# Weight conversion during the attention: intermediate words in a PSUM bank, high halves on GpSimd

## The chip, the cores and the metric

The kernel runs on one core of a Trainium2 chip. The metric is the device time of one execution in microseconds (us); lower is better. The kernel before takes 1587.08 us, the median of 3 runs (1586.88 to 1588.7).

## The reference

Three stages follow each other: an attention with hashed buckets, a feed-forward layer with a rational activation, and eight experts weighted by a normalised gate. The weights w_in and w_out of the second stage arrive as 64-bit floats, because a 32-bit array is multiplied by a 64-bit scalar when they are set up.

```python
def _attn_ref(q, k, v, proj):
    mask = q_bucket[:, :, :, None] == k_bucket[:, :, None, :]
    scores = np.where(mask, scale * np.matmul(q, k.transpose(0, 1, 3, 2)), -1e9)
    attn = np.exp(scores - np.max(scores, axis=-1, keepdims=True))
    attn = attn / (np.sum(attn, axis=-1, keepdims=True) + 1e-09)
    return np.matmul(attn, v).astype(np.float32)
...
def _moe_ref(x, w_in, w_out, a, b):
    h = x @ w_in
    P = a[0] + a[1] * h + a[2] * h * h + a[3] * h * h * h
    Q = 1.0 + np.abs(b[0]) * np.abs(h) + np.abs(b[1]) * h * h
    return ((P / (Q + 1e-06)) @ w_out).astype(np.float32)
```

## The kernel before

Every fp32 operand is split into a high half (fp32r) and a low half (the rest), and a product is three matmuls: high by high, high by low, low by high.

**The attention** (L683 to L762) runs 48 iterations: 16 heads, each with 3 groups of 256 query rows. An iteration issues two `scores` (TensorE into the two-bank tiles of `ps_s`, then VectorE L285 takes the row minimum out of PSUM and ScalarE L286 the exponential), three `trans` (four TensorE transposes L308 into a one-bank tile `pt`, a ScalarE copy of the high half into `pth` by L106, a VectorE subtraction into `ptl` by L109), one `values` (twelve matmuls L323 into a one-bank tile `av`, ScalarE L106 and VectorE L334 take it out), and `norm` (VectorE L291 and L292, GpSimd L294). Once per head `prep_head_a` fills four one-bank tiles `tp` (taken out by ScalarE L246) and `prep_head_b` two one-bank tiles `hp` (taken out by VectorE L260, which writes the mask bits). All of `tp`, `hp`, `pt` and `av` come from the same four PSUM banks: `bank(name)` at L89 has one tag with `bufs=4`, and per head they are 18 tiles.

**The weight conversion** of a 64-bit weight tile of 128x512 numbers (`prep_weights` L188, path `one`) has these steps: ScalarE takes the absolute value of the upper words into `c` (L169), GpSimd clips it (L170), VectorE builds two 32-bit floats out of the raw words in four steps (`narrow_b`, L180 to L183), GpSimd adds them into `c` (L186), ScalarE copies the high half of `c` into the weight slot (L208, by the helper `act_copy` at L106), and GpSimd writes the low half (L210, by `pool_lo` at L103). The tile `c` has two buffers (`conv`, L87), so the L169 of one conversion waits until the last step (L103) of the conversion two before has read `c`.

Thirty-two tiles are converted: eight during the attention (the dictionary `wprep` at L718 places them at iterations 35, 38, 41 and 44, one of w_in and one of w_out each), the other 24 during the second stage. The flag `bits_in_psum` tells the two apart: it is False for the eight (L719) and True for the 24 (L784). During the second stage the intermediate words `pc` lie in the PSUM bank `sum_bank(3, "bits")`; during the attention `pc` is `c` itself.

**What orders the work.** During the attention a planner orders each engine's instructions: an instruction's rank is its place in the program, and one that is ready when its engine would otherwise idle, by the planner's own estimate of times, is taken ahead of its place if its tile can be had. So the eight conversions are spread over the first 215 us although the program places them at iterations 35 to 44. From L806 on (`manual_schedule`) the order is the one that is written. Each engine executes its queue in order. The second stage starts with `gemm1` (L354) on the first four pairs of converted weights.

Of the kernel before, what the change touches and what calls it, by code (L numbers as in the profile page):

```python
# [35 lines left out]
def kernel(  # L36
# [52 lines left out]
    def bank(name):  # L89
        return ps.tile([P, 512], F32, tag="b", bufs=4, name=name)  # L90
# [4 lines left out]
    def split(eng_hi, eng_lo, hi, lo, src):  # L95
        eng_hi(hi, src)
        eng_lo(lo, src, hi)
# [4 lines left out]
    def pool_lo(lo, src, hi):  # L102
        pool.tensor_tensor(lo, src, hi.bitcast(F32), ALU.subtract)  # L103

    def act_copy(o, src):
        act.activation(o, src, AF.Copy)  # L106
# [38 lines left out]
    def load_weights(m, c):  # L145

        if c >= (NA_W if wide else NA_W // 2) + E * EF // 2:
            return
        if c < NA_W and wide:
            src, f, nf = (moe_w_in, moe_w_out)[m].bitcast(I32), c, 1  # L150
        elif c < NA_W // 2 and not wide:
            src, f, nf = (moe_w_in, moe_w_out)[m], 2 * c, 2
        else:
            e, f = divmod(2 * (c - (NA_W if wide else NA_W // 2)), EF)
            src, nf = (w1, w2)[m][e], 2
        w = 2 // nf if src.dtype == I32 else 1
        if m == 0:
            r = raw.tile([P, KC, 2 * P], src.dtype, tag="ra", name="ra")
            sp.dma_start(r, src[:, f * P * w:(f + nf) * P * w].rearrange("(c p) f -> p c f", p=P))
        else:  # L160
            r = raw.tile([P, nf, 2 * DM // nf], src.dtype, tag="rb", name="rb")
            sp.dma_start(r, src[f * P:(f + nf) * P, :].rearrange("(f p) d -> p f d", p=P))
        raws[m, c] = r

    def narrow_a(bits):


        c = conv.tile([P, bits.shape[1]], F32, tag="c", name="c")
        act.activation(c, bits[:, :, 1].bitcast(F32), AF.Abs)  # L169
        pool.tensor_scalar(c, c, F64_HIGH, F64_LOW, ALU.min, ALU.max)  # L170
        return c

    def narrow_b(bits, c):


        ci = c.bitcast(I32)
        pc = sum_bank(3, "bits") if bits_in_psum else c
        pi = pc.bitcast(I32)
        low, high = bits[:, :, 0], bits[:, :, 1]
        dve.tensor_scalar(pi, ci, 5, 2, ALU.logical_shift_left, ALU.logical_shift_right)  # L180
        dve.scalar_tensor_tensor(high, high, -0x40000000, pi, ALU.bitwise_and, ALU.bitwise_or)
        dve.tensor_scalar(pi, high, -0x800000, None, ALU.bitwise_and)
        dve.scalar_tensor_tensor(low.bitcast(F32), low.bitcast(U32), 2.0 ** -52, pc, ALU.mult, ALU.mult)  # L183

    def narrow_c(bits, c):
        pool.tensor_tensor(c, bits[:, :, 0].bitcast(F32), bits[:, :, 1].bitcast(F32), ALU.add)  # L186

    def prep_weights(m, i):  # L188

        if i >= NW:  # L190
            return
        one = wide and i < NA_W
        c, j = (i, 0) if one else divmod(i - NA_W, 2) if wide else divmod(i, 2)
        if wide and not one:
            c += NA_W
        r = raws[m, c]
        t = wslots[(i % NSLOT) // 4].tile([P, 2, 512], F32R, tag=f"w{'ab'[m]}{i % NSLOT}", name="w" + "ab"[m])
        slots[m, i] = tuple(t[:, k].rearrange("p (c f) -> p c f", c=KC) if m == 0 else t[:, k] for k in range(2))
        if one:
            bits = (r.rearrange("p c f -> p (c f)") if m == 0 else r[:, 0]).rearrange("p (n t) -> p n t", t=2)  # L200
            n = narrow_a(bits)
            yield
            narrow_b(bits, n)
            yield
            narrow_c(bits, n)
            load_weights(m, c + 2)
            yield
            act_copy(t[:, 0], n)  # L208
            yield
            pool_lo(t[:, 1], n, t[:, 0])  # L210
            return
        if m == 0:
            split(pool_hi, pool_lo, t[:, 0].rearrange("p (c f) -> p c f", c=KC),
                  t[:, 1].rearrange("p (c f) -> p c f", c=KC), r[:, :, j * P:(j + 1) * P])
        else:
            split(pool_hi, pool_lo, t[:, 0], t[:, 1], r[:, j])
        if j == 1:
            load_weights(m, c + 2)
# [500 lines left out]
    bits_in_psum = False  # L719
    for it in range(NG + VLAG):  # L720
# [39 lines left out]
        if it in wprep:  # L760
            for m in range(2):
                list(prep_weights(m, wprep[it]))  # L762
# [11 lines left out]
    def sum_bank(j, name):  # L774

        return ps_f.tile([P, 512], F32, tag="f" if j < 3 else "c", bufs=3 if j < 3 else 1, name=name)
# [7 lines left out]
    bits_in_psum = True  # L784
# [21 lines left out]
    with tc.manual_schedule(engines={mybir.EngineType.PE, mybir.EngineType.Activation, mybir.EngineType.DVE,  # L806
# [3 lines left out]
        for s in range(NS + QF):  # L810
            n = s - NS
# [19 lines left out]
            if n < 0:  # L831
                go(new)
            narrowing = [prep_weights(m, i) for m, i in preps.get(s, ())]
            narrowing = [w for w in narrowing if go(w)]
            for w in old_w:
# [116 lines left out]
```

## Time and profile before

| | |
|---|---|
| median of 3 runs | 1587.08 us |
| the profiled execution | 1589.4 us, of which the span is 1587.6 us |
| TensorE busy | 1536.8 us (97%) |
| VectorE busy | 1199.3 us (76%) |
| ScalarE busy | 622.1 us (39%) |
| GpSimd busy | 938.9 us (59%) |
| mean granted TensorE clock | 0.994 |

The attention takes the first 290 us of the span, the second stage goes on to about 575 us, the experts take the rest. The busy shares are averages over these stages: VectorE is nearly full in the first and the second and is idle for about a third of the last. What the change is worth must therefore be read from the first 290 us alone: from the timeline of each engine, from the windows, and from the distance between the same step of successive heads.

### The profile page before, as it was taken

Reading aid. Unit: us, or ns where it says so; the run is one execution under the profiler, and the core shown is the slowest. Engines: PE = TensorE matmul, PEld = TensorE weight load, DVE = VectorE, ACT = ScalarE, POOL = GpSimd, SP = SyncE. Lnnn points to the kernel's source line nnn. Section 1 sums busy time; section 2 is a strip of 40 time slices with the busy share of each in tenths; the row PEclk is TensorE's granted clock in tenths of the full one; section 3 lists DMA queues with packets and bytes.
Section 4 is the critical chain, followed back from the end, with each engine's and each line's share of the span. In section 5 each row is a group of like instructions: output and inputs, shape, how many; then the busy total and the mean of one; then the engine's idle time right before and its main releaser. Section 6 shows DMA issues by size and latency. Waiting matters only on the chain.

```text
span 1587.6 us, 22241 instructions
## 1 busy us (share of the span) xinstructions
PE 1536.8 (97%) x8071; PEld 1355.8 (85%) x8071; DVE 1199.3 (76%) x2116; ACT 622.1 (39%) x1167; POOL 938.9 (59%) x1165
## 2 busy tenths in 40 slices
PE   5989999899999999999999999999999999999999
PEld 4888889687777877889899999989899998989898
DVE  7989999799999984886666766676666666666665
ACT  4878888788777842111111111111111111111111
POOL 6777875577777976456644653564465356436530
PEclk8999999999999999999999999999999999999999
DMA  5322221021212000101010110101011001101002
GB/s 170 86 83 79 81 70 25 14 67 54 66 53 67 14 27 27 41 27 40 27 41 27 41 40 27 36 32 40 27 40 41 27 28 40 40 27 40 14 1 80
DMA packets 49406, 71.85 MB, mean 45 GB/s; under 512 B 4368, under 2 KB 35088, under 8 KB 49296
## 3 DMA queue, kind: packets, MB, share of 16 engines
q1 hardware_dynamic: 48432, 68.85, 14.1%
q8 instruction: 64, 1.05, 0.3%
q10 hardware_dynamic: 864, 1.57, 0.3%
q14 instruction: 46, 0.38, 0.1%
HBM read 59.79 MB, written 3.15 MB: 40 GB/s over the span
## 4 chain that ended last, share of the span: by engine, by line
PE 65%; DVE 2%; ACT 0%; issue 0%; DVEq 0%; ACTq 0%
PE accb L599 33%; PE prod L534 29%; PE acca L405 2%; PE h L354 1%; PE lp L635 0%; DVE t L470 0%; DVE t L473 0%; DVE c L559 0%; DVE part L417 0%; DVE gl L555 0%; ACT xb L106 0%; DVE t L480 0%; ACT gh L554 0%; DVE t L484 0%; DVE csum L676 0%
## 5 line engine op out<-in xcount | busy, mean ns | idle before, releaser
L534 PE MATMUL prod<-xb,ww 128*128 128x384 f32 x2688 | 481.7, 336 | 1.8 <-ACT m L106 1.3
L599 PE MATMUL accb<-wb,gh 128*128 128x512 f32 x1536 | 475.7, 391 | 2.9 <-ACT osum L106 2.5
L534 PEld LDWEIGHTS prod<-xb,ww 128*128 128x128 f32 x2688 | 469.8, 188 | 8.0 <-ACT m L106 1.6
L610 DVE SCALAR_TENSOR_TENSOR osum<-accb,gp,osum 128x512 f32<-128x512 f32 x336 | 251.7, 749 | 127.7 <-PE accb L599 126.0
L599 PEld LDWEIGHTS accb<-wb,gh 128*128 128x128 f32 x1536 | 287.0, 188 | 60.9 <-ACT osum L106 2.9
L599 PE MATMUL accb<-wb,gl 128*128 128x512 f32 x768 | 300.9, 392 | 0.4 <-DVE gl L555 0.4
L100 POOL TENSOR_SCALAR wb<-rb 128x512 fp32r<-128x512 f32 x64 | 40.2, 627 | 405.8 <-PE accb L599 405.8
L554 ACT ACTIVATE gh<-c 128x384 fp32r<-128x384 f32 x256 | 134.3, 526 | 352.5 <-DVE c L559 352.1
L106 ACT ACTIVATE m<-prod 128x384 f32<-128x384 f32 x64 | 31.5, 492 | 457.9 <-PE prod L534 457.9
L599 PEld LDWEIGHTS accb<-wb,gl 128*128 128x128 f32 x768 | 144.2, 188 | 32.0 <-DVE gl L555 1.7
L555 DVE SCALAR_TENSOR_TENSOR gl<-c,gh 128x384 fp32r<-128x384 f32 x256 | 165.2, 645 | 1.3 <-ACT gh L554 0.9
L559 DVE TENSOR_TENSOR c<-prod,u 128x384 f32<-128x384 f32 x192 | 106.6, 558 | 61.7 <-PE prod L534 54.1
L354 PE MATMUL h<-xh,wa 128*128 128x512 f32 x384 | 126.7, 392 | 3.4 <-DVE tu L377 3.4
L405 PE MATMUL acca<-gh,wb 128*128 128x512 f32 x384 | 126.4, 391 | 2.8 <-DVE part L417 1.7
L109 DVE TENSOR_TENSOR ptl<-pt,pth 128x512 fp32r<-128x512 f32 x144 | 94.5, 682 | 19.1 <-ACT pth L106 18.3
L559 DVE TENSOR_TENSOR c<-prod,m 128x384 f32<-128x384 f32 x64 | 35.7, 558 | 92.4 <-PE prod L534 92.4
L103 POOL TENSOR_TENSOR ww<-ra,ww 128x256 fp32r<-128x256 f32 x128 | 95.4, 746 | 10.7
L294 POOL TENSOR_SCALAR e<-e,rs 128x768 f32<-128x768 f32 x96 | 88.8, 937 | 20.8 <-DVE rs L292 11.3
L308 PE MATMUL pt<-idr,e 128*128 128x128 f32 x576 | 83.0, 279 | 11.1 <-DVE ptl L109 4.9
L285 DVE TENSOR_SCALAR_CACHE_REDUCE e<-s 128x768 f32<-128x768 f32 x96 | 90.9, 949 | 2.1 <-PE s L278 1.7
L286 ACT ACTIVATE e<-e,nm 128x768 f32<-128x768 f32 x96 | 89.9, 936 | 3.8 <-DVE e L285 3.1
L354 PEld LDWEIGHTS h<-xh,wa 128*128 128x128 f32 x384 | 72.1, 188 | 22.4 <-DVE tu L377 5.9
(168 smaller groups left out, 2546.3 us busy)
## 6 DMA issues: line engine op xcount, KB each, us to landing
ra<-in_moe_w_dram SPq DMA_DIRECT2D x32, 512.0 KB
rb<-in_moe_w_dram SPq DMA_DIRECT2D x32, 512.0 KB
ra<-in_moe_w_in_dram SPq DMA_DIRECT2D x16, 512.0 KB
rb<-in_moe_w_out_dram SPq DMA_DIRECT2D x16, 512.0 KB
qkv<-in_q_dram SPq DMA_DIRECT2D x16, 192.0 KB
qkv<-in_k_dram SPq DMA_DIRECT2D x16, 192.0 KB
qkv<-in_v_dram SPq DMA_DIRECT2D x16, 192.0 KB
a<-a SPq DMA_DIRECT2D x16, 192.0 KB
```

Source lines behind the costliest of these rows:

```text
L103: pool.tensor_tensor(lo, src, hi.bitcast(F32), ALU.subtract)
L109: dve.tensor_tensor(lo, src, hi.bitcast(F32), ALU.subtract)
L285: dve.tensor_scalar(e[j], s[:, 0:S], BIG, None, ALU.min, ALU.min, accum_out=nm)
L286: act.activation(e[j], e[j], AF.Exp, bias=nm, scale=-1.0, accum_out=rs[:, j, 0:1])
L354: pe.matmul(hps, lhsT=a[:, c], rhs=x[:, c], start=m == 0, stop=m == 3 * KC - 1)
L405: pe.matmul(o, lhsT=l[:, js], rhs=r, start=f == 0 and m == 0, stop=f == QF - 1 and m == 2)
L534: pe.matmul(o, lhsT=w[:, i, c], rhs=x[:, j, c], start=n == 0, stop=n == 5)
L554: act.activation(gh, c, AF.Relu)
L555: low.append(lambda: dve.scalar_tensor_tensor(gl, c, 0.0, gh.bitcast(F32), ALU.max, ALU.subtract))
L559: dve.tensor_tensor(c, o, x, ALU.add)
L599: pe.matmul(o, lhsT=l[:, ts], rhs=r, start=n == 0 and m == 0, stop=n == 1 and m == 2)
L610: dve.scalar_tensor_tensor(d, o, gate["p"][:, n, e:e + 1], d, ALU.mult, ALU.add)
```

## The change

Two expressions change, and both act only while `bits_in_psum` is False, that is for the eight conversions during the attention. The intermediate words `pc` of `narrow_b`, which L180 writes, L181 reads, L182 writes again and L183 reads, lie in a tile of `bank("bits")`, one of the four banks that `tp`, `hp`, `pt` and `av` share, and no longer in `c`. And the high half of the converted tile is written by `pool_hi` (L100, GpSimd) where it was written by `act_copy` (L106, ScalarE).

```diff
         ci = c.bitcast(I32)
-        pc = sum_bank(3, "bits") if bits_in_psum else c
+        pc = sum_bank(3, "bits") if bits_in_psum else bank("bits")
         pi = pc.bitcast(I32)
...
-            act_copy(t[:, 0], n)
+            (act_copy if bits_in_psum else pool_hi)(t[:, 0], n)
             yield
             pool_lo(t[:, 1], n, t[:, 0])
```

## Rows read from the trace of the kernel before

**Rows 1.** Windows: stretch; busy us (count) per engine; granted clock, DMA share, GB/s.
```profile
240.00:260.00 20.00, 20.00 (x150) 18.09 (x149) 17.47 (x41) 17.77 (x38) 12.51 (x16) 1.00 0.19 45
...
285.00:300.00 15.00, 14.98 (x80) 12.63 (x81) 7.74 (x13) 8.37 (x15) 6.79 (x9) 1.00 0.00 1
```

**Rows 2.** Timeline (start us, us, instruction), VectorE: first mask-bit step of ten heads.
```profile
92.93 1.29 DVE L260 TENSOR_SCALAR bits<-hp,thr 44x512 fp32r<-44x512 f32 x2
...
110.95 1.29 DVE L260 TENSOR_SCALAR bits<-hp,thr 44x512 fp32r<-44x512 f32 x2
...
130.63 1.29 DVE L260 TENSOR_SCALAR bits<-hp,thr 44x512 fp32r<-44x512 f32 x2
...
146.75 1.29 DVE L260 TENSOR_SCALAR bits<-hp,thr 44x512 fp32r<-44x512 f32 x2
...
164.68 1.29 DVE L260 TENSOR_SCALAR bits<-hp,thr 44x512 fp32r<-44x512 f32 x2
...
180.79 1.29 DVE L260 TENSOR_SCALAR bits<-hp,thr 44x512 fp32r<-44x512 f32 x2
...
197.60 1.29 DVE L260 TENSOR_SCALAR bits<-hp,thr 44x512 fp32r<-44x512 f32 x2
...
212.81 0.82 DVE L260 TENSOR_SCALAR bits<-hp,thr 44x512 fp32r<-44x512 f32 x1
...
229.83 1.29 DVE L260 TENSOR_SCALAR bits<-hp,thr 44x512 fp32r<-44x512 f32 x2
...
260.51 1.29 DVE L260 TENSOR_SCALAR bits<-hp,thr 44x512 fp32r<-44x512 f32 x2
```

**Rows 3.** Timeline, four engines, one conversion's end; the last line another's.
```profile
111.41 0.63 ACT L106 ACTIVATE wa<-c 128x512 fp32r<-128x512 f32 x1 [2.50 <-POOL c L186]
...
112.11 1.29 POOL L103 TENSOR_TENSOR wa<-c,wa 128x512 fp32r<-128x512 f32 x1 [0.74 <-ACT wa L106]
...
113.44 0.69 ACT L169 ACTIVATE c<-ra 128x512 f32<-128x512 f32 x1 [0.48 <-POOL wa L103]
...
114.63 0.69 DVE L109 TENSOR_TENSOR ptl<-pt,pth 128x512 fp32r<-128x512 f32 x1 [2.40 <-ACT pth L106]
...
115.47 0.63 PE L308 MATMUL pt<-idr,e 128*128 128x128 f32 x4 [1.45 <-DVE ptl L109]
...
213.98 0.63 ACT L106 ACTIVATE wb<-c 128x512 fp32r<-128x512 f32 x1 [2.29 <-POOL c L186]
```

**Rows 4.** Windows, as rows 1: one microsecond after that end.
```profile
118.00:119.00 1.00, 1.00 (x5) 0.90 (x5) 1.00 (x4) 0.00 (x0) 0.00 (x0) 0.50 0.00 0
```

**Rows 5.** Windows, only instructions on tile c, then (300:520) on bits.
```profile
13.00:26.00 13.00, 8.19 (x8) 1.40 (x3) 5.25 (x5) 0.84 0.57 146
...
30.00:300.00 270.00, 22.17 (x24) 7.84 (x12) 17.61 (x18) 0.98 0.24 67
...
300.00:520.00 220.00, 66.28 (x96) 1.00 0.18 58
```

**Rows 6.** Line view: count, ns min/median/max, first and last start, form.
```profile
L180 DVE TENSOR_SCALAR c<-c x8: 405/893/1220, 13.6 to 177.7; 128x512 int32<-128x512 int32 x8
...
L100 POOL TENSOR_SCALAR wb<-rb x64: 617/619/922, 550.8 to 1523.9; 128x512 fp32r<-128x512 f32 x64
```

**Rows 7.** Timeline, TensorE: a wait at the start of the attention.
```profile
25.22 0.79 PE L277 MATMUL s<-b,a 128*128 128x512 f32 x1 [3.51 <-DVE e L285]
```

**Rows 8.** Timeline, TensorE and VectorE: banks' first writers, last readers; one conversion's span.
```profile
88.35 1.03 PE L308 MATMUL pt<-idr,e 128*128 128x128 f32 x8
...
90.85 0.39 PE L259 MATMUL hp<-a,pjr 128*108 128x256 f32 x2
...
91.55 1.28 DVE L109 TENSOR_TENSOR ptl<-pt,pth 128x512 fp32r<-128x512 f32 x2
...
107.81 0.89 DVE L180 TENSOR_SCALAR c<-c 128x512 int32<-128x512 int32 x1
...
141.34 1.42 DVE L183 SCALAR_TENSOR_TENSOR rb<-rb,c 128x512 f32<-128x512 uint32 x1
```

## The prediction

> **What bounds the kernel now.** The change touches only the eight conversions of the attention, so I read that stage and the way its end reaches the total. First the windows view: where the attention runs without conversions (240 to 260 us) TensorE is busy for all of the 20 us, VectorE for 17.47 and GpSimd for 12.51 [rows 1]; TensorE sets the pace there, with VectorE close behind. At the hand-over to the second stage (285 to 300 us) TensorE is busy for 14.98 of 15 us [rows 1]: the second stage's matmuls follow the attention's without a gap, and all they need of this stage is the attention's result and weights that are ready long before. So a microsecond won or lost in the attention reaches the end one for one.
>
> Second, the pace. The first mask-bit step of each head (L260) is a mark that comes once a head [rows 2]. From 229.83 to 260.51, with no conversion at work, two heads take 30.68 us, 15.34 each. With conversions the heads fall in two kinds. Five take 18.02, 19.68, 17.93, 16.81 and 17.02 us, 89.46 together, 17.89 each. Three others take 16.12, 16.11 and 15.21, 15.81 each [rows 2]. So a conversion costs about 0.5 us in a head of the second kind and 2.1 us more in one of the first.
>
> Third, the timeline of the engines shows what the first kind has. ScalarE comes to the copy of the high half (L106, wa<-c) and waits 2.50 us for GpSimd's sum (L186); the exponentials and pth copies stand behind it in its queue. Then VectorE waits 2.40 us for pth, and TensorE waits 1.45 us for VectorE to give back a bank [rows 3]. There are five such waits between 91 and 214 us, the last of 2.29 us [rows 3], one in each of the five slow heads. Behind the one shown TensorE's granted clock falls to 0.50, that is 1.2 of its 2.4 GHz [rows 4], after TensorE had been idle; that is in the head of 19.68 us.
>
> **The change, part by part.**
>
> *The copy leaves ScalarE.* Eight copies of 0.63 us [rows 3] and their waits for L186 go; the step follows L186 on the same engine. In the heads of 16.81 and 17.02 us nothing else of a conversion stands on ScalarE. They should fall to the pace of the second kind: 33.83 - 2 x 15.81 = 2.2 us won. In the other three, L169 of a later conversion stands soon behind the copy and waits for GpSimd's last step L103 on the same buffer of c (0.48 us in the row [rows 3]). ScalarE now comes to that L169 up to 2.5 us earlier, while L103 ends about as late as before, so a part of the wait only moves there. The three heads have 55.63 - 3 x 15.81 = 8.2 us over the second kind; the bounds are nothing and 8.2, and I take half, 4.1 us, because nothing in the trace says how the planner spaces the two.
>
> *The copy comes to GpSimd.* Eight more instructions; the same operation on the same shape takes 0.62 us there [rows 6], 5.0 us together. They displace the 0.74 us in which GpSimd waits for ScalarE ahead of L103 [rows 3], up to 5.9 us if all eight have it. I take 0, with -1 and +5 as bounds: GpSimd is idle for 7.5 of 20 us in the clean window [rows 1], but its norm step L294 is queued behind the conversion and TensorE's transposes wait for that.
>
> *The words move to PSUM.* The second stage already does these four VectorE steps with pc in PSUM: 96 of them take 66.28 us, 0.69 each [rows 5]. During the attention, in SBUF, 24 take 22.17 us, 0.92 each, and the first eight 8.19 us, 1.02 each [rows 5]. So VectorE is relieved of 22.17 - 24 x 0.69 = 5.6 us and, at the start, of 8.19 - 8 x 0.69 = 2.7 us. VectorE is not alone on the path; the heads of the second kind lie 15.81 - 15.34 = 0.47 us over the clean pace, 4.7 us in ten heads, and that bounds what shorter steps can return there. I take 2.5 us (bounds 0 and 4.7). At the start TensorE waits 3.51 us for VectorE's L285 [rows 7] while VectorE works on conversions, so I count 2.0 of the 2.7 us there (bounds 0 and 2.7).
>
> The row also shows what is given up: the shortest L180 in SBUF took 0.405 us, while the median is 0.893 [rows 6]. The Trainium skill says why (VectorE: DVE Perf Modes, section Why PSUM operands drop a tier): a one-input step reads through both SBUF ports at twice the rate, and with an operand in PSUM fp32 drops to the plain rate. By that rule alone the 16 one-input steps would be longer by 0.28 us each, an estimate of 4.5 us lost. The same notes (SBUF — State Buffer, section Who interferes with whom) say that both kinds of SBUF step share ports with GpSimd and block each other; the spread of the row, 0.405 to 1.220 us for one form, agrees, and the measured means decide.
>
> *One bank of four is taken away for a time.* This is the price. The tile bits holds a bank from L180 to the end of L183. In the trace of before one conversion spreads these four steps from 107.81 to 142.76 us, 35 us [rows 8], since VectorE's queue has few holes; five conversions go like this. If the order stayed, 5 x 35 = 175 us would run on three banks, about 10.5 heads. What that can cost: two transposes start at 88.35 us, and their banks are read by ptl from 91.55 on, the first free at 92.19. The fourth tile in use, hp, starts at 90.85 us, while an earlier hp, which L260 reads from 92.93 us on, is still held [rows 2, 8]. With three banks it would wait 1.34 us. Such a wait in each of a head's three iterations is 4.0 us, 42 us in 10.5 heads. The other bound is nothing: the planner knows of the bank, VectorE gets more holes when banks are short, and the conversion then runs through sooner; and TensorE has the score matmuls, in other banks, to go on with. I take 0.4 us a head, 4.2 us, nearer to nothing, because the hold of a pt is mostly waiting in the queues of ScalarE and VectorE, which these changes shorten. The new wait of L180 for its bank is cheap where VectorE itself was the bank's last reader (14 of the 18 tiles of a head); behind a tp it would stop VectorE's queue until ScalarE's L246 is done. The first matmul of the tile that follows in the bank waits for L183, and all of TensorE's queue behind it.
>
> **The sum.** -2.0 (start) - 2.2 (two heads) - 4.1 (three heads) - 2.5 (shorter steps) + 0 (GpSimd) + 4.2 (bank) = -6.6 us. Against the profiled execution, 1589.4 us (span 1587.6 and 1.8 around it), that is 1582.8; that execution lies 2.3 us over the median of the runs, 1587.08, and against the median it is 1580.5 us.
>
> **The rivals.**
>
> *The bank decides, and it is slower.* If three banks cost 1.5 us a head, the 10.5 heads lose 15.8 us against 10.8 won: +5.0, 1592.1 us. It decides from 10.8 / 10.5 = 1.03 us a head on. For it speaks that all four banks were in use in the example and that TensorE's waits in the slow heads end on VectorE's ptl [rows 3, 8]; against it that a wait of 1.34 us arises only where tiles stand as close as there. The Trainium skill speaks for it (Perfetto Trace Analysis, section Matmuls): independent groups should rotate through different banks, so that emptying one overlaps the next group's matmuls; the trace agrees in so far as pt, av and hp overlap in this way.
>
> *The wait only moves.* ScalarE waits at L169 instead of at the copy, and the three heads keep their 8.2 us: -2.0 - 2.2 - 2.5 + 4.2 = -2.5 us, 1584.6 us. For it speaks that L169 waited for L103 already [rows 3].
>
> *All of the waits go and the bank is free.* -2.0 - 2.2 - 8.2 - 2.5 = -14.9 us, 1572.2 us: the heads come near to the clean pace of 15.34 us. For it speaks that VectorE has 2.5 of 20 us to spare there [rows 1].
>
> *The change does nothing at the end*, because the second stage hides it: the hand-over speaks against that [rows 1], and I give it no chance of its own.
>
> **How the numbers follow.** The forecast, 1580.5 us, has 0.48; the slower rival 0.23; the moved wait 0.17; the full gain 0.12. The measurement tells 0.2%, about 3.2 us, from no change. The forecast and the full gain are faster, 0.60; the moved wait is within, 0.17; slower 0.23. The range goes from just below the full gain, 1571.5, to just over the slower rival, 1592.5; beyond it lies about half of the slower case's chance, and little below. The cases of the faster sign alone would have 1572 to 1583.
>
> **What would show it.** Right: no wait of ScalarE for L186; the VectorE steps at 0.69 us; L260 marks at 15.3 to 16.5 us a head; no clock of 0.5 between 40 and 280 us. Wrong on the bank: waits of TensorE for L183, or for ptl, xp and the mask bits, in every head, and head distances over 16.6 us where a bits tile lives. Wrong on the moved wait: ScalarE idle for 1 to 2.5 us ahead of L169. Wrong on GpSimd: TensorE's transposes waiting longer for L294 behind L100. The planner may also put the whole stage in another order; waits at places that neither edit touches would make the sum meaningless.

## The result and the profile after

The changed kernel takes 1597.51 us (median of 6 runs, 1595.35 to 1598.62) against 1587.64 us before: a ratio of 1.006, interval 1.0047 to 1.0073. It is slower by 9.9 us where 6.6 us of gain were forecast, and it lies outside the range of 1571.5 to 1592.5 us. The profiled execution is 1597.56 us with a span of 1595.8, so span goes with span: 1587.6 before, 1595.8 after.

The first view to read is again the mark of each head, VectorE's first mask-bit step. From the third mark on, in the kernel after:

```profile
37.00 1.29 DVE L260 TENSOR_SCALAR bits<-hp,thr 44x512 fp32r<-44x512 f32 x2
...
53.00 1.29 DVE L260 TENSOR_SCALAR bits<-hp,thr 44x512 fp32r<-44x512 f32 x2
...
175.55 1.29 DVE L260 TENSOR_SCALAR bits<-hp,thr 44x512 fp32r<-44x512 f32 x2
...
190.98 1.29 DVE L260 TENSOR_SCALAR bits<-hp,thr 44x512 fp32r<-44x512 f32 x2
...
213.95 1.29 DVE L260 TENSOR_SCALAR bits<-hp,thr 44x512 fp32r<-44x512 f32 x2
...
238.61 1.29 DVE L260 TENSOR_SCALAR bits<-hp,thr 44x512 fp32r<-44x512 f32 x2
...
261.74 1.29 DVE L260 TENSOR_SCALAR bits<-hp,thr 44x512 fp32r<-44x512 f32 x2
```

From the fourth mark (53.00 us) to 190.98 us nine heads take 15.2 to 15.4 us each, the clean pace of before. 190.98 is the thirteenth mark; the thirteenth of before stands at 212.81 [rows 2]. So the changed kernel is 21.8 us ahead there. Then four stretches follow that it did not have before: the next three heads take 22.97, 24.66 and 23.13 us, and one more such stretch comes behind the sixteenth mark. The second stage's first matmul, before and after:

```profile
290.03 0.39 PE L354 MATMUL h<-xh,wa 128*128 128x512 f32 x1
...
296.65 0.40 PE L354 MATMUL h<-xh,wa 128*128 128x512 f32 x1
```

So all of the 21.8 us is lost again, and 6.6 more. (The spans differ by 8.2 us; the last 1.6 arise behind the attention and were not followed.)

VectorE's timeline shows what these stretches hold (they are called bursts below), the first of the four here:

```profile
199.66 0.68 DVE L180 TENSOR_SCALAR bits<-c 128x512 int32<-128x512 int32 x1
...
200.33 0.67 DVE L180 TENSOR_SCALAR bits<-c 128x512 int32<-128x512 int32 x1
200.91 0.68 DVE L181 SCALAR_TENSOR_TENSOR ra<-ra,bits 128x512 int32<-128x512 int32 x1
201.50 0.68 DVE L181 SCALAR_TENSOR_TENSOR rb<-rb,bits 128x512 int32<-128x512 int32 x1
202.10 0.69 DVE L182 TENSOR_SCALAR bits<-ra 128x512 int32<-128x512 int32 x1
202.70 0.68 DVE L182 TENSOR_SCALAR bits<-rb 128x512 int32<-128x512 int32 x1
203.29 0.68 DVE L183 SCALAR_TENSOR_TENSOR ra<-ra,bits 128x512 f32<-128x512 uint32 x1
203.89 0.68 DVE L183 SCALAR_TENSOR_TENSOR rb<-rb,bits 128x512 f32<-128x512 uint32 x1
...
212.77 0.16 DVE L291 TENSOR_REDUCE rs<-rse 128x2 f32<-128x4 f32 x1 [4.08 <-ACT e L286]
```

Both weights of a pair are converted at once, in two banks, with no other long step between (left out is a 0.15 us reciprocal). The other bursts start at 224.02, 248.54 and 270.66 us. Before, the eight conversions were spread from 13.6 to 177.7 us [rows 6] and one took 35 us [rows 8]; now they stand where the program places them. GpSimd, ScalarE and TensorE in the first burst:

```profile
205.22 1.04 POOL L186 TENSOR_TENSOR c<-ra 128x512 f32<-128x512 f32 x1
206.34 0.62 POOL L100 TENSOR_SCALAR wa<-c 128x512 fp32r<-128x512 f32 x1
206.92 1.04 POOL L186 TENSOR_TENSOR c<-rb 128x512 f32<-128x512 f32 x1
207.92 1.27 POOL L103 TENSOR_TENSOR wa<-c,wa 128x512 fp32r<-128x512 f32 x1
209.17 0.61 POOL L100 TENSOR_SCALAR wb<-c 128x512 fp32r<-128x512 f32 x1
209.86 1.27 POOL L103 TENSOR_TENSOR wb<-c,wb 128x512 fp32r<-128x512 f32 x1
...
212.39 1.19 POOL L170 TENSOR_SCALAR c<-c 128x512 f32<-128x512 f32 x2
214.02 1.79 POOL L294 TENSOR_SCALAR e<-e,rs 128x768 f32<-128x768 f32 x2 [0.43 <-DVE rs L292]
...
209.23 0.67 ACT L169 ACTIVATE c<-ra 128x512 f32<-128x512 f32 x1 [2.40 <-POOL wa L103]
211.16 0.66 ACT L169 ACTIVATE c<-rb 128x512 f32<-128x512 f32 x1 [1.26 <-POOL wb L103]
211.73 0.92 ACT L286 ACTIVATE e<-e,nm 128x768 f32<-128x768 f32 x1
...
213.90 0.50 PE L277 MATMUL s<-b,a 128*128 128x512 f32 x1 [3.44 <-DVE e L285]
```

Read it as a chain, by times. GpSimd works without a hole from 205.22 to 211.13 us on the pair. ScalarE's L169 of the next pair waits for its low halves (2.40 and 1.26 us: the wait of [rows 3] at its new place), and an exponential is queued behind. VectorE's row sum L291 waits 4.08 us for that exponential, and behind L291 stands the score reduction L285, for which TensorE waits 3.44 us. The clips L170 of the next pair come behind this row (212.39 us), and then the norm. The windows give the price in clock too (stretch; busy us (count) of PE, PEld, DVE, ACT, POOL; granted clock, DMA share, GB/s):

```profile
175.55:190.98 15.43, 15.36 (x118) 13.99 (x117) 14.03 (x32) 13.29 (x28) 12.13 (x16) 1.00 0.26 70
...
212.00:214.00 2.00, 0.10 (x1) 0.11 (x1) 1.19 (x5) 1.34 (x4) 1.50 (x3) 1.00 0.01 4
214.00:216.00 2.00, 1.81 (x9) 1.37 (x10) 1.94 (x4) 1.67 (x4) 1.79 (x2) 0.81 0.00 0
216.00:218.00 2.00, 2.00 (x12) 2.00 (x11) 1.97 (x5) 1.00 (x3) 1.13 (x2) 0.50 0.20 37
```

TensorE does 0.10 us of work in 212 to 214 us, and at 216 to 218 us its granted clock is 0.50, that is 1.2 GHz, while it is busy throughout.

### The profile page after: what moved, and what is told of

The parts are those of the page before. It is cut to its first block, busy times and chain, and to the rows that moved or that the text cites. A ratio compares the mean times of both kernels' runs of the same rounds, so it can differ in the third digit from the quotient of the medians.

```text
span 1595.8 us, 22260 instructions
## 1 busy us (share of the span) xinstructions
PE 1541.7 (97%) x8071; PEld 1360.3 (85%) x8071; DVE 1191.7 (75%) x2116; ACT 620.1 (39%) x1159; POOL 935.6 (59%) x1173
## 4 chain that ended last, share of the span: by engine, by line
PE 64%; DVE 3%; ACT 1%; issue 0%; DVEq 0%; ACTq 0%
PE accb L599 32%; PE prod L534 28%; PE acca L405 2%; PE h L354 1%; PE lp L635 0%; DVE t L470 0%; DVE t L480 0%; ACT xb L106 0%; DVE t L473 0%; DVE c L559 0%; DVE part L417 0%; DVE gl L555 0%; ACT gh L554 0%; DVE xb L109 0%; DVE t L484 0%
## 5 line engine op out<-in xcount | busy, mean ns | idle before, releaser
L100 POOL TENSOR_SCALAR wb<-rb 128x512 fp32r<-128x512 f32 x64 | 40.2, 627 | 407.1 <-PE accb L599 407.1
L106 ACT ACTIVATE m<-prod 128x384 f32<-128x384 f32 x64 | 31.5, 492 | 458.2 <-PE prod L534 458.2
L294 POOL TENSOR_SCALAR e<-e,rs 128x768 f32<-128x768 f32 x96 | 86.2, 910 | 29.6 <-DVE rs L292 19.4
L285 DVE TENSOR_SCALAR_CACHE_REDUCE e<-s 128x768 f32<-128x768 f32 x96 | 91.1, 950 | 3.6 <-PE s L278 3.2
L308 PE MATMUL pt<-idr,e 128*128 128x128 f32 x576 | 87.2, 286 | 6.6 <-DVE ra L183 3.0
```

The costliest lines, as they stand in the source:

```text
L285: dve.tensor_scalar(e[j], s[:, 0:S], BIG, None, ALU.min, ALU.min, accum_out=nm)
```

## The experiments

Each time is the median; the number behind it is its difference from the median of the kernel before that was measured along with it (1588.32 to 1588.81 us), then the ratio with its interval. The experiments are called e1, e2 and so on. In every one the planner makes a new order, so a difference in time can be the edit's own or the new order's.

**Each edit alone.** First the copy alone (e1): the kernel before with L208 as after.

```diff
-            act_copy(t[:, 0], n)
+            (act_copy if bits_in_psum else pool_hi)(t[:, 0], n)
```

> The second half of the change alone: the high half of the eight conversions on GpSimd, the words still in c. Theory (place in the queue): the changed kernel lost because its words lie in a tile of the shared bank tag, so that the planner may not take the conversions ahead of their place in the program and they come as four bursts; GpSimd's copy is harmless. Then here the conversions stay spread over 13 to 215 us as in the kernel before, no ScalarE wait for L186 is left, and the time is 1575 to 1586 us. Rival (GpSimd is overloaded by the copy): heads of 17 us and more with TensorE waiting for L294, 1590 us or more.

Measured: 1593.48 us, +5.2, 1.0034 (1.0021 to 1.0047). The conversions stay spread, as the theory said, but the time is the rival's; the rival's wait is not there, since TensorE's waits for the norm L294 are 4.2 us from 40 to 300 us and were 4.5 before. Three readings. The head of the last conversion takes 17.06 us (marks at 215.19 and 232.25) and took 17.02 us before [rows 2], although ScalarE's wait of 2.29 us [rows 3] is gone. GpSimd's timeline, e1's first and the kernel before's behind it, shows why:

```profile
215.30 1.05 POOL L186 TENSOR_TENSOR c<-rb 128x512 f32<-128x512 f32 x1
216.44 0.62 POOL L100 TENSOR_SCALAR wb<-c 128x512 fp32r<-128x512 f32 x1
217.14 1.28 POOL L103 TENSOR_TENSOR wb<-c,wb 128x512 fp32r<-128x512 f32 x1
218.41 1.78 POOL L294 TENSOR_SCALAR e<-e,rs 128x768 f32<-128x768 f32 x2
...
212.91 1.04 POOL L186 TENSOR_TENSOR c<-rb 128x512 f32<-128x512 f32 x1
214.69 1.28 POOL L103 TENSOR_TENSOR wb<-c,wb 128x512 fp32r<-128x512 f32 x1 [0.74 <-ACT wb L106]
215.95 1.79 POOL L294 TENSOR_SCALAR e<-e,rs 128x768 f32<-128x768 f32 x2
```

From sum to norm are 3.11 us in e1 and 3.04 us before: the copy fills the hole in which GpSimd waited, the norm L294 comes as late as ever, and the head is as long as ever. The head of 16.81 us is 17.02 in e1, likewise.

The second reading: in the other three slow heads ScalarE's wait moved to L169, as the rival "the wait only moves" had it. There are waits of 3.20, 4.26 and 3.21 us, one in each; the longest:

```profile
116.67 0.67 ACT L169 ACTIVATE c<-ra 128x512 f32<-128x512 f32 x1 [4.26 <-POOL wa L103]
```

These heads take 18.01, 19.02 and 17.99 us, 55.0 together, where they took 55.63 [rows 2]. So the five slow heads are not where e1 loses, and taking the copy from ScalarE won next to nothing in them.

The third reading is where e1 loses. Its fourth mark is at 64.24 us where that of before is at 61.53, its sixth at 96.08 where that of before is at 92.93, and from there to the sixteenth mark e1 is 0.7 us the faster. (Its span is 4.0 us longer, of which 1.6 us arise behind the attention.) In the stretch ahead of the fourth mark e1's VectorE and GpSimd have

```profile
43.55 1.20 DVE L180 TENSOR_SCALAR c<-c 128x512 int32<-128x512 int32 x1 [3.12 <-POOL c L170]
...
42.90 0.61 POOL L170 TENSOR_SCALAR c<-c 128x512 f32<-128x512 f32 x1
```

and the kernel before

```profile
55.92 1.61 DVE L180 TENSOR_SCALAR c<-c 128x512 int32<-128x512 int32 x2
...
43.05 0.61 POOL L170 TENSOR_SCALAR c<-c 128x512 f32<-128x512 f32 x1
```

The clip L170 comes no later than before. What differs is the order: the planner put L180 12 us earlier in VectorE's queue, where the clip, behind the copy, the low half and a norm on GpSimd, is not done yet. TensorE waits 3.4 us for the ptl behind this L180. So the loss goes with the order that was planned for the copy on GpSimd; that the copy's own 0.62 us would cost anything in the old order is not shown.

Then the bank alone (e2): the kernel before with `pc` as after.

```diff
-        pc = sum_bank(3, "bits") if bits_in_psum else c
+        pc = sum_bank(3, "bits") if bits_in_psum else bank("bits")
```

> The first half of the change alone: the words in a tile of the shared bank tag, the high half still on ScalarE. Theory (place in the queue): the same four bursts at 190 to 280 us, heads of 23 to 25 us there and 15.3 us before them; 1593 to 1603 us, a little more than the changed kernel since ScalarE also waits for L186. Rival (GpSimd is overloaded by the copy): without the copy the loss is gone, 1580 to 1588 us.

Measured: 1587.31 us, -1.0, 0.9993 (0.9985 to 1.0002). The four bursts are there (from 198.70 us on), so it is the bank that makes them; but the time is the rival's. The thirteenth mark is at 190.02 us; then the heads take 20.2, 21.1 and 20.5 us, about 5 us over the clean pace each where the changed kernel has 7.6 to 9.3. ScalarE's copy still waits for the sum, as before, but now the L169s do not wait, and exponentials run in between:

```profile
205.33 0.63 ACT L106 ACTIVATE wa<-c 128x512 fp32r<-128x512 f32 x1 [2.30 <-POOL c L186]
...
207.00 0.93 ACT L286 ACTIVATE e<-e,nm 128x768 f32<-128x768 f32 x1
...
208.40 0.67 ACT L169 ACTIVATE c<-ra 128x512 f32<-128x512 f32 x1
...
209.88 0.66 ACT L169 ACTIVATE c<-rb 128x512 f32<-128x512 f32 x1
```

**Is it the shared tag that makes the bursts?** The changed kernel with a bank of its own for `bits`, and three for the rest (e3):

```diff
-        return ps.tile([P, 512], F32, tag="b", bufs=4, name=name)
+        return ps.tile([P, 512], F32, tag="b", bufs=3, name=name)
...
-        pc = sum_bank(3, "bits") if bits_in_psum else bank("bits")
+        pc = sum_bank(3, "bits") if bits_in_psum else ps.tile([P, 512], F32, tag="bits", bufs=1, name="bits")
```

> The whole change, but the words lie in a bank with a tag of its own, and three banks are left for tp, hp, pt and av throughout. Theory (place in the queue): free of the shared tag the conversions are spread over 13 to 215 us again; the three banks cost at most 0.5 us a head; 1574 to 1588 us. Rival (the missing bank is what costs, the mechanism of the prediction's slower case): TensorE waits for ptl, xp or the mask bits in every head, heads of 16.8 us or more in all of the attention, 1592 us or more.

Measured: 1603.29 us, +15.0, 1.0097 (1.0081 to 1.0112). VectorE's conversion steps are spread again, from 13.41 to 147.77 us: yes, the tag. It also prices a bank, and there the theory's 0.5 us a head was too little; the time is the rival's. With no conversion left, the first and the last of seven marks:

```profile
168.45 1.29 DVE L260 TENSOR_SCALAR bits<-hp,thr 44x512 fp32r<-44x512 f32 x2
...
272.01 1.29 DVE L260 TENSOR_SCALAR bits<-hp,thr 44x512 fp32r<-44x512 f32 x2
```

Six heads take 103.56 us, 17.26 each instead of 15.34: three banks cost 1.9 us a head, with the order that was planned for three. TensorE's waits that the waits view names there, for L285, are 4.5 us in all, less than half of the 11.5; what makes up the rest is not settled.

**What makes a burst dearer with the copy on GpSimd?** First more work on GpSimd, less on ScalarE (e4): |x| by two GpSimd steps, so that L169 is gone.

```diff
-        act.activation(c, bits[:, :, 1].bitcast(F32), AF.Abs)
+        if bits_in_psum:
+            act.activation(c, bits[:, :, 1].bitcast(F32), AF.Abs)
+        else:
+            x = bits[:, :, 1].bitcast(F32)
+            pool.tensor_scalar(c, x, 0.0, 2.0, ALU.max, ALU.mult)
+            pool.tensor_tensor(c, c, x, ALU.subtract)
```

> The changed kernel, but the absolute value of the upper words (L169) of the eight conversions is taken by two GpSimd steps (twice the positive part, less the number), so that ScalarE has no part in these conversions and can't wait for c. VectorE's order is the same as in the changed kernel, bursts included. Theory (in a burst most of the loss is ScalarE's wait at L169 for the buffer of c, with the exponentials behind it): heads with a burst fall from 23 to 25 us to 17.5 to 20.5 us, 1580 to 1589 us. Rival (the burst on VectorE and the two banks it holds are the loss): the heads stay at 22 us or more, 1594 us or more.

Measured: 1615.72 us, +27.4, 1.0175 (1.0162 to 1.0189). The waits view of TensorE from 188 to 300 us (us in total, times, longest; L299 is the norm, since the lines shift):

```profile
PE pt L313 <- POOL e L299: 26.3, 7, 8.8
```

ScalarE waits for no c there, and two of the heads take 30 us. The time is in the rival's range, but the cause is neither's: with more for GpSimd to do ahead of the norm, TensorE waits 26.3 us for it, where it waits 1.2 us in the changed kernel.

Then L169's wait for the low half away (e8): the sum L186 is written over the raw upper words, so c is free once L180 has read it. The next load of raw words moves behind the low half.

```diff
-        pool.tensor_tensor(c, bits[:, :, 0].bitcast(F32), bits[:, :, 1].bitcast(F32), ALU.add)
+        s = c if bits_in_psum else bits[:, :, 1].bitcast(F32)
+        pool.tensor_tensor(s, bits[:, :, 0].bitcast(F32), bits[:, :, 1].bitcast(F32), ALU.add)
+        return s
...
-            narrow_c(bits, n)
-            load_weights(m, c + 2)
+            n = narrow_c(bits, n)
+            if bits_in_psum:
+                load_weights(m, c + 2)
...
             pool_lo(t[:, 1], n, t[:, 0])
+            if not bits_in_psum:
+                load_weights(m, c + 2)
```

> The changed kernel, bursts included, but L186 writes its sum over the raw upper words and the two halves are taken from there, so that c is free after L180 and the next conversion's L169 has not to wait for L103; GpSimd's steps and their order stay. Theory (in the changed kernel the loss against the bank alone is ScalarE's wait at L169, with the exponentials behind it): no such wait, heads with a burst 19.5 to 21.5 us as with the bank alone, 1583 to 1590 us. Rival (GpSimd's row of conversion steps is itself in the way, and the norm L294 stands behind it): heads of 22 us or more, 1594 us or more.

Measured: 1592.16 us, +3.5, 1.0018 (1.0009 to 1.0027), between the theory's range and the rival's. So this edit gives back 6.4 of the 10.9 us between the changed kernel (+9.9) and the bank alone (-1.0). It does more than take the wait away. With c free the L169s of the next pair stand at 200.19 and 201.50 us, between the steps of this pair and not behind its low halves (209.23 and 211.16 us in the changed kernel), and GpSimd's clips come up with them, ahead of the pair's sums:

```profile
202.26 0.61 POOL L170 TENSOR_SCALAR c<-c 128x512 f32<-128x512 f32 x1
...
203.55 0.61 POOL L170 TENSOR_SCALAR c<-c 128x512 f32<-128x512 f32 x1
```

In the changed kernel they stand behind the low halves. So 6.4 and 4.5 us are what two edits give, not the shares of two causes in the changed kernel. For the remaining 4.5 us these clips, 0.61 us of GpSimd's work in each conversion, are taken out of this kernel (e14):

```diff
-        pool.tensor_scalar(c, c, F64_HIGH, F64_LOW, ALU.min, ALU.max)
+        if bits_in_psum:
+            pool.tensor_scalar(c, c, F64_HIGH, F64_LOW, ALU.min, ALU.max)
```

> The kernel with GpSimd's sum written over the raw words (so that ScalarE's L169 no longer waits), and now without GpSimd's clip of the absolute value (L170) in the eight conversions of the attention: the clip is a part of the computation that is left out, 0.61 us of GpSimd each. It tells whether what is left of the loss in the four bursts is GpSimd's row of work ahead of the norm step, on which TensorE's transposes wait. Theory (GpSimd's row is the path in a burst): two clips less in each row, 1.2 us earlier norm in each of three to four bursts, 1592.2 falls by 3.6 to 5 us to 1587 to 1588.5, and the norm stands 1.2 us earlier after the burst's first VectorE step. Rival (VectorE's eight steps back to back are the path, GpSimd only follows): no change, 1591.5 to 1592.5.

Measured: 1587.13 us, -1.7, 0.999 (0.9981 to 0.9999), as the theory said. Less GpSimd work in the bursts gives 5.2 us back. GpSimd's timeline, the norm of the first burst in e14 (its line is L300), then in e8 (L299), and TensorE's waits for the norm from 188 to 300 us, in the same order:

```profile
211.29 1.80 POOL L300 TENSOR_SCALAR e<-e,rs 128x768 f32<-128x768 f32 x2
...
214.04 1.79 POOL L299 TENSOR_SCALAR e<-e,rs 128x768 f32<-128x768 f32 x2
...
PE pt L314 <- POOL e L300: 0.6, 1, 0.6
...
PE pt L313 <- POOL e L299: 5.9, 7, 3.0
```

GpSimd has no hole in either from the sums to this norm, and VectorE's eight steps were done by 204.5 us in both: the norm follows GpSimd's row. Counted from the thirteenth mark, this is where the norm of the first burst stands, with the time of the three heads behind the mark:

| kernel | norm, us behind the mark | three heads, us | against before, us |
|---|---|---|---|
| bank alone (e2) | 21.3 | 61.8 | -1.0 |
| e14 | 21.5 | 62.5 | -1.7 |
| the changed kernel | 23.0 | 70.8 | +9.9 |
| e8 | 23.3 | 68.0 | +3.5 |
| e4 | 28.9 | 78.9 | +27.4 |

An early norm goes with the shorter heads, a late one with the longer. e8, its norm as late as the changed kernel's, takes less; there L169's wait for the low half is gone.

The same clip taken out of the first experiment's kernel, where the conversions are spread (e15):

> The kernel before with the high half of the eight on GpSimd (words still in c), and without GpSimd's clip (L170) in the eight conversions, which is a part of the computation that is left out. The copy had brought 8 x 0.62 us to GpSimd and cost 5.2 us (1593.5 against 1588.3); leaving out the clips takes 8 x 0.61 us from it again. Theory (the amount of GpSimd's work in the spread conversions sets the loss): back to 1587.5 to 1589.5. Rival (the loss comes from ScalarE's wait at L169 for the low half, which the clip does not change): 1592 to 1593.5.

Measured: 1585.84 us, -3.0, 0.9983 (0.9974 to 0.9991), 8.1 us less than with the clip. That is more than the theory's bound and more than the 4.9 us of the clips themselves. The rival's time is wrong, and so is its premise: ScalarE's waits at L169 for the low halves change too, from 3.20, 4.26 and 3.21 us to 2.12, 2.71 and 2.71 (an earlier one from 0.91 to 1.53). But the amount of GpSimd's work is not shown to be the cause either. TensorE's waits for the norm are 5.8 us (4.2 in e1), and most of the gain is there by the third mark (42.84 against 46.92 us), where VectorE's order is another one: with the clip its wait for it goes (the 3.12 us above). What the copy costs by itself in spread conversions stays open.

**Spread with the bank.** Where the program itself places single conversions apart, the bank need not mean bursts (e5):

```diff
-    wprep = {NG - 13 + 3 * j: j for j in range(QF)}
+    wprep = {5 + 5 * n: divmod(n, 2) for n in range(2 * QF)}
...
-            for m in range(2):
-                list(prep_weights(m, wprep[it]))
+            j, m = wprep[it]
+            list(prep_weights(m, j))
```

> The changed kernel (bank and GpSimd copy) with the eight conversions placed one at a time at iterations 5, 10, 15 to 40 of the program and not in pairs at 35, 38, 41 and 44. Theory (the bursts are the loss; one conversion alone fits into what VectorE and GpSimd have to spare in a head): heads of 15.3 to 16.2 us throughout, no wait of ScalarE at L169, 1568 to 1578 us. Rival (a conversion costs its time wherever it stands, because its four VectorE steps in a row and its bank stop TensorE): eight heads of 17.5 us or more, 1583 to 1595 us.

Measured: 1587.83 us, -0.8, 0.9993 (0.9984 to 1.0003): the gain did not come, and the time is the rival's. The heads take 15.7 to 19.3 us, where the changed kernel has nine clean ones and then long ones. The same with ScalarE's copy kept (e10):

> As the kernel with single conversions at iterations 5 to 40, but the high half stays on ScalarE (bank alone). Theory (bursts): 1568 to 1580 us; ScalarE waits up to 2 us for L186 in some heads, so not below the one with the copy on GpSimd by more than 2 us. Rival (GpSimd's copy is what costs, here too): 4 us or more below the one with the copy on GpSimd.

Measured: 1586.61 us, -2.1, 0.9986 (0.9977 to 0.9995), neither the theory's gain nor the rival's 4 us. How much can be won at most is told by a kernel that leaves the eight conversions out, so that the first four weight pairs are constants (e7; its sixteen memsets, 0.52 to 0.53 us each on GpSimd, stay):

```diff
+            if not bits_in_psum:
+                pool.memset(t[:, 0].bitcast(F32), 0.5)
+                pool.memset(t[:, 1].bitcast(F32), 0.5)
+                load_weights(m, c + 2)
+                return
```

> The kernel before without the eight conversions of the attention: their weight tiles are set to a constant by GpSimd memsets, so the first four pairs of weights of the second stage are not the reference's; all else runs. It shows what the conversions cost in all: from the clean heads of 15.3 us the attention should end about 25 us earlier, 1558 to 1568 us.

Measured: 1566.74 us, -21.9, 0.9863 (0.9849 to 0.9877), its heads from the fourth mark on at 15.2 to 15.5 us. So the conversions cost 21.9 us in the kernel before, 20.9 with the bank alone, 31.8 in the changed kernel. VectorE's part of one is 4 x 0.69 = 2.76 us, 22 us in eight, and a clean head leaves VectorE 15.43 - 14.03 = 1.4 us. That 22 is near 21.9 proves nothing: in the kernel before these steps take 30.4 us [rows 5], and the last run below pays 17.1 us with the same 22. The bank's clean heads were no gain: the same cost was put off.

The last two, spread and with the sum written over the raw words (the diffs of e5 and e8 together), first the changed kernel (e11), then the one with ScalarE's copy (e12):

> The changed kernel with one conversion at a time at iterations 5, 10, ... 40 (instead of two at 35, 38, 41, 44), and the sum written over the raw words. Spread alone gave 1587.8, with ScalarE still waiting up to 3.4 us at L169. Theory (the wait at L169 and GpSimd's row share the loss, and single conversions leave GpSimd idle time to do its row): without that wait 1583 to 1586.5. Rival (the eight conversions cost about VectorE's 2.76 us each in heads that leave it 1.4 us, whatever ScalarE waits for): 1587 to 1588.5, as with the wait.

Measured: 1587.22 us, -1.6, 0.9989 (0.998 to 0.9998), as its rival said.

> The kernel before with the words in a bank, the high half by ScalarE, one conversion at a time at iterations 5, 10, ... 40, and the sum written over the raw words. Without the last part it took 1586.6, and ScalarE waited 5.2 us in five copies for the sum and up to 1.8 us at L169. Theory (waits at L169 are on the path): 1584 to 1586. Rival (the eight conversions cost VectorE's time in every case): 1586 to 1587.5.

Measured: 1583.94 us, -4.9, 0.9969 (0.9956 to 0.9981): better than both kernels, just under the theory's range, and 17.1 us for the conversions. ScalarE's copies wait for the sum as long as ever, 8.5 us in seven copies (in e10 they are 8.2 us in eight, where the expectation has 5.2 in five); those into wa:

```profile
ACT wa L106 <- POOL ra L187: 4.6, 3, 2.3
```

The gain over e10, 2.8 us, comes with L169's wait of up to 1.8 us going; that this wait is all of it is argued, not shown. Against it speaks that e11 loses a longer wait, up to 3.4 us, and gains 0.8 us over e5, which is not clear of the noise. TensorE's waits for the norm from 40 to 300 us fall from 3.0 to 1.0 us between e10 and e12, and grow from 5.4 to 6.4 between e5 and e11: with the copy on GpSimd the norm comes no sooner.

## Why the prediction was wrong

**The bank.** The step that failed first is "If the order stayed, 5 x 35 = 175 us would run on three banks", and with it the sum, whose terms are taken from spread conversions. The order did not stay: the shared tag held the eight conversions at their place in the program (e2, e3), the first step at 199.66 us instead of 13.61, and four bursts gave back the 21.8 us that nine clean heads had won, and 6.6 more. The price a head that the step went with, 0.4 us, was too small as well: a bank that is missing throughout costs 1.9 us (e3), above the 1.03 us from which the slower rival was to decide. The rival's page (the Trainium skill, Perfetto Trace Analysis, section Matmuls, on rotating through different banks) agrees with e3: with one bank less to rotate through a head takes 17.26 instead of 15.34 us. But its mechanism is not what made the changed kernel slower: nothing runs with fewer banks for long there, a pair holds its two for 4.9 us, and TensorE's waits for L183 are 3.0 us in all. The rival had the sign right, and by luck. The last paragraph of the prediction named another order as possible and gave it no price.

**ScalarE's waits as the cause of the slow heads.** "They should fall to the pace of the second kind: ... 2.2 us won" is wrong in its reason. The wait for L186 was in each slow head, but so was GpSimd's row of sum, low half and norm, and in these two heads that row set the end: 17.02 and 17.06 us in e1 against 16.81 and 17.02. The 4.1 us of the other three heads came to 0.6 in e1, where the wait moved to L169. A wait that occurs in every slow head was taken for its cause without asking what GpSimd does in it.

**GpSimd's copy at 0 (-1 to +5).** The reason given, that it fills the 0.74 us in which GpSimd waits, holds in the row of e1's last head. Spread, the kernel with it costs 5.2 us (e1, just over the bound), in an order in which L180 waits for L170; the prediction had no such path, and the copy's own part in it is open. In bursts it costs 10.9 us (the changed kernel against e2): the two copies make GpSimd's row longer, ScalarE's L169 waits for the end of the row, and the norm comes 1.7 us later. e8 and e14 give all of it back, by taking that wait away and then the clips out of the row; how the 10.9 us divide between the two paths in the changed kernel is not shown. The prediction had both mechanisms, one as the rival "the wait only moves" and one as "behind the conversion and TensorE's transposes wait for that", but sized them for spread conversions.

**The start.** -2.0 was taken. The third mark moved from 45.19 to 37.00 us, -8.2, because no conversion is left there (37.37 us in e7, which has none at all). It is a delay and not a gain: the changed kernel still pays for the eight, later.

**VectorE's steps.** 0.67 to 0.69 us each, as taken from the second stage's rows [rows 5]. The clean pace of the full-gain case was met for nine heads, and paid for in the four bursts. The premise that a microsecond of the attention reaches the end one for one held: without the conversions the second stage's first matmul comes 23.2 us earlier (266.87 against 290.03 us), and the span is 23.2 us shorter (1564.4 against 1587.6).

## What to carry to other kernels

Where a scheduler hoists work, a temporary's pool is part of the schedule: a tile from a pool that the neighbours rotate through can pin the work to its place in the program, so compare the order of the instructions before any durations. Work that goes to the most idle engine by average is not free if its queue holds a step on which the bound engine waits; read what stands between it and that step, in spread work and in a burst. And measure a kernel without the moved work: it tells a gain from a delay.

## What was not expected of the hardware

Two things, both small. The step L180, which took 0.405 to 1.220 us in SBUF [rows 6], takes 0.67 to 0.69 us in the bursts with the words in PSUM, GpSimd at work beside it: it never reaches the short time and never the long one. And in this stretch the clock fell behind the idle time, not in it: it was 1.00 while TensorE did 0.10 us of work (212 to 214 us), 0.81 in the next two microseconds and 0.50 in the two after, with TensorE busy again, so the idle time went on costing when it was over.
